# A linear-attention and FFN kernel: float32 numerators on column halves of the array, and the key side and the denominators turned through DRAM

## The chip, the cores and the metric

One core of a Trainium2 chip runs the whole program. The metric is the device time of one execution in microseconds (us); lower is better.

## What is computed

```python
def phi(x):
    proj = np.einsum('bhsd,md->bhsm', x, omega)
    sq = np.sum(x * x, axis=-1, keepdims=True) / 2.0
    h = proj - sq
    h = h - np.max(h, axis=-1, keepdims=True)
    return np.exp(h) / np.sqrt(m)
q_p, k_p = phi(q * scale), phi(k * scale)
kv = np.einsum('bhsm,bhsd->bhmd', k_p, v)
z = np.sum(k_p, axis=2)
num = np.einsum('bhsm,bhmd->bhsd', q_p, kv)
den = np.einsum('bhsm,bhm->bhs', q_p, z)[..., None] + 1e-06
attn = num / den                       # 8 batches, 8 heads, 576 tokens, 64 wide, 128 features
x = attn.transpose(0, 2, 1, 3).reshape(4608, 512)
h = x @ w_in                           # 512 x 2048
return (h - np.tanh(h)) @ w_out        # 2048 x 512
```

## The kernel before

The 4608 tokens are cut into eleven chunks of 256, 256, 256, 384, 384 and six times 512. For each chunk the FFN runs over 16 slices of 128 hidden columns: `h` (12 matmuls, L541), tanh on ACT (L815), a subtraction on DVE (L816), a split of the result into a high and a low part (L817 on ACT, L818 on DVE), and 3 matmuls for each of the chunk's 128-token blocks into `po` (L564 to L566). Every product of full accuracy in the FFN is made of three passes in `float32r`, a one-pass format: high by high, high by low, low by high.

The attention of a later chunk is woven into the FFN of an earlier one. Heads are handled in pairs, c = 0 to 3, two heads of 64 rows side by side in 128 partitions. Three kinds of units make it:

- Batches 0 to 2 and chunks 0 to 2 go through `native_k` and `native_q`, in plain float32, in the first part of the program (the table `ORDER`). `native_q.pn` (L1019) multiplies two heads into the two column halves of the array, rows 0 to 63 and 64 to 127 of one PSUM bank.
- Each batch b = 3 to 7 and pair c is a `k_unit` (20 in all). It makes the features of the keys, splits them and the values, and adds up kv transposed in a bank `pk`. Then it sums z per partition on DVE (`zA` to `zl`, L732 to L749), and PE turns both: `kt` (L760, L762) makes two transposes, and two matmuls against ones that add z up over the partitions and spread it over all of them. `ka`, `kb` and `zb` read that back out of PSUM, `wa` and `wv` split kv into two halves for the numerators.
- Each chunk 3 to 10 and pair c is a `q_unit` (32 in all), written `q<chunk><pair>` in the tables. Per 128-token block it projects (`p`, L593), copies and reduces (`c`, `t`), takes the exponential (`e`, L612) and sums the denominators (`d`, L623). Then `r` takes the reciprocal, `n` multiplies the features by it on ACT (L632), `tr` turns 32 x 32 blocks on DVE (L635), four DMAs `dw` write them to DRAM and two DMAs `dr` read them back with tokens along the free axis (L641, L644). Per head, `a` (L654, ACT) and `l` (L658, DVE) split the features into a high and a low part, `m` (`numerators`) makes the products, and `ta` (L670, ACT) and `tv` (L674, DVE) add the two parts of the product into `xs`, the chunk's input to the FFN. `xh` and `xl` split that into `xa`.

A chunk crosses a batch edge at most once (576 tokens are four and a half blocks), so `numerators` runs over one or two pieces of a chunk, and per piece and head it makes two `float32r` matmuls, one of `qh` and one of `ql`, each with all 128 columns of `kvw` (64 of the high part of kv, 64 of the low).

The order of all work is written out by hand in two tables, `ORDER` and `LATER`; a token is `unit.step.slot`, and each engine runs its instructions in that order. `LATER` begins near 170 us. SP issues nearly all DMAs, one after the other; a DMA that has to wait holds up those behind it. Engines: PE matmuls, DVE and ACT elementwise work, SP the DMAs.

Of the kernel before, what the change touches and what calls it, by code (L numbers as in the profile page):

```python
# [9 lines left out]
F32 = mybir.dt.float32  # L10
# [43 lines left out]
k23.exp5.1 q11.pt1.4 k13.kvwa k13.kvwd k00.pk0.2 k11.red5 q11.qt1.1 k10.lk.1 q01.nA1 k11.redB q11.pn.7 k11.redA  # L54
# [5 lines left out]
k10.exp5.1 d0.di k23.kvwa k23.zb k12.pj.1.7.5 q01.qt0.1 q10.expB.7 k23.kvwd k01.z k01.zt q10.expA.4 k12.redB  # L60
# [28 lines left out]
f0f.h0.6 f0e.gl q31.ld k30.sv0 q30.c0.0 f0f.h1 k30.sv1 k30.vhA0.0 k30.vhA1.1 q30.t0 k31.ld q30.e0 k30.vlA0 q30.p1.4  # L89
k30.vlA1 q30.p2.7 q30.d0 k30.pA0.0 f0f.th f0e.o0 x.h0 f0f.g x.h1 f0e.o1 x.h2 x.l0 f0f.gh x.l1 f0e.o2 x.l2 x.h3 f0f.gl  # L90
q30.c1 f0e.o3 q30.c2 q31.sa x.l3 q30.t1 f20.h0.6 q30.t2 q30.e1 q31.sv q30.e2 f20.h1 k30.cA0.0 q30.d1 q32.ld q30.d2
k30.tA0 q31.p0.4 f20.th q31.p1.7 q30.r q31.p2.0 q30.n0 f0f.o0 f20.g q30.n1 f0f.o1 q30.tr0 f20.gh q30.tr1 f0f.o2 s0.c0.2
s0.c1.3 q30.dw0 f0f.o3 q31.c0.1 q30.dw1 f20.gl s0.c2.1 s0.d0 f21.h0.6 q31.c1 s0.d1 q31.t0 q31.c2 s0.d2 q31.e0 s0.c3.0
q30.dw2 q30.dw3 q32.sa q31.d0 s0.d3 f21.h1 q31.t1 q31.t2 q31.e1 q32.sv q31.e2 k30.pA1.4 k30.pM.7 f20.o0.2 f21.th q31.d1
q33.ld k30.eA0 f21.g k30.cA1 f20.o1.3 q30.dr0 q31.d2 k30.cM.0 f21.gh q30.dr1 k30.khA0.0 q31.r k30.tA1 q31.n0 f21.gl
f22.h0.6 q31.n1 q31.tr0 k30.eA1 q31.tr1 k30.klA0 f22.h1 q31.dw0 k30.khA1.1 q31.dw1 k30.tM k30.klA1 q30.a0 q31.dw2
k30.zA.0 q31.dw3 k30.eM q30.l0 f21.o0 f22.th k30.zA2 k30.zM f22.g f21.o1 f22.gh f22.gl q30.m0.0 k30.pB0.4 q30.ta0.2
# [12 lines left out]
k30.kb k31.klA1 q33.dr1 k30.wa f27.h1 k31.khM.0 k30.wv k31.klM k31.vlM k31.zA.0 k31.zA2 q32.m1.7 f27.th k31.zM q40.p0.4  # L110
k31.kvA1 q30.xh f27.g k31.kvM f26.o0 q31.xh q30.xl q40.c0.0 f27.gh q31.xl q33.a0 q40.t0 f26.o1 q40.e0 f27.gl k31.vhB0.0
q33.l0 k31.vhB1.1 q40.p1.4 q32.ta1 q40.d0 f30.h0.6 k31.vlB0 q40.c1 k31.vlB1 q40.t1 k32.lv q40.e1 q32.tv1 q33.m0.4
q40.d1 q32.xh q40.p2.7 q33.a1 q32.xl q40.c2 q33.l1 q41.sa q40.t2 q41.sv q33.m1.7 q33.ta0.0 q33.ta1 q33.tv0 q40.e2
q42.ld q40.d2 q41.p0.4 q41.c0.1 q33.tv1 q40.r q33.xh q41.p1.7 q41.t0 q40.n0 q33.xl q41.p2.4 q40.n1 q40.tr0 f30.h1
q41.e0 q40.tr1 q41.c1 q41.d0 f27.o0 q40.dw0 q41.c2 q41.t1 q40.dw1 f30.th q40.dw2 q41.t2 q41.e1 q40.dw3 f30.g q41.e2
f27.o1 q41.d1 f30.gh q41.d2 s2.c0.2 f30.gl k31.pB0.7 q42.sa s2.c1.3 s2.d0 k31.pB1.4 f31.h0.6 q41.r s2.d1 q42.sv q41.n0
f31.h1 q41.n1 q40.dr0 q41.tr0 k31.cB0.0 q40.dr1 k31.cB1 f30.o0.2 q41.tr1 q43.ld f31.th k31.tB0 k32.sa q41.dw0 f30.o1.3
f31.g q41.dw1 f30.o2.1 q41.dw2 k31.tB1 q41.dw3 k32.sv0 f31.gh f32.h0.6 k31.eB0 f31.gl q40.a0 f32.h1 k31.khB0.0 k31.eB1
k32.sv1 f31.o0 q40.l0 k33.ld f32.th k31.klB0 f31.o1 f32.g q40.m0.7 q41.dr0 k31.khB1.1 f32.gh k31.zB.0 q41.dr1 k31.kvB0
f31.o2 k31.klB1 q40.a1 f32.gl k32.vhA0.0 k31.kvB1 q40.ta0.1 q40.l1 f33.h0.6 k32.vhA1.1 q40.tv0 k31.zB2 k32.vlA0 f33.h1  # L120
k31.ca.0 k32.vlA1 k31.zM2 k31.cv q40.m1.4 k31.zh.0 f33.th k31.zl q42.p0.7 q41.a0 f32.o0 f33.g q42.c0.0 q41.l0 f32.o1
# [248 lines left out]
def favor_attention_ffn(ctx: ExitStack, tc: tile.TileContext, qT, kT, va, vt, omT, w, out):  # L370
# [202 lines left out]
    def q_unit(ch, c):  # L573
# [75 lines left out]
        def rows_of(x):  # L649
            return x.rearrange("p (t a j) -> p t a j", a=4, t=T)  # L650
# [559 lines left out]
```

## Time and profile before

| what | us |
|---|---|
| three runs | 1016.25, 1025.86, 1025.47 (median 1025.47) |
| the profiled execution | 1017.37 |
| its span, first to last instruction | 1015.6 |

Around the profiled span lie 1.8 us that no instruction fills. The profile is of one execution; what a row calls busy is the union of its instructions, and a matmul's listed duration contains the time in which its results drain, so that matmuls that follow each other overlap. The time from one matmul's start to the next one's start is what it takes of PE.

### The profile page before, as it was taken

What the parts mean: (1) busy time and instruction counts of PE and PEld (TensorE: products, weight loads), DVE (VectorE), ACT (ScalarE), POOL (GpSimd) and SP (SyncE); (2) the same over time, 40 slices, a digit from 0 to 9 for tenths busy, and PEclk for the clock granted to TensorE, in tenths of its full rate; (3) what the DMA queues carried; (4) which work ended last, traced back from release to release, by engine and by line L of the source; (5) the groups of instructions that cost most, each with busy time, mean ns of one, the idle gap of its engine ahead of it and who ended that gap; (6) DMA issues with size and microseconds to landing.
All of it is one profiled execution on the core that took longest, in us unless ns stands there. A gap on an engine that the chain in (4) does not pass through costs nothing.

```text
span 1015.6 us, 16915 instructions
## 1 busy us (share of the span) xinstructions
PE 993.8 (98%) x5260; PEld 839.8 (83%) x5260; DVE 802.5 (79%) x2844; ACT 730.3 (72%) x1905; POOL 49.5 (5%) x77
## 2 busy tenths in 40 slices
PE   8999999989999999999999999999999999999998
PEld 7878778978889888888887888888888888888886
DVE  6999778998999999999998998898898638424222
ACT  8997668888888887888887886877778638323222
POOL 1334330000000000000000000000000000000000
PEclk9999999999999999999999999999999999999999
DMA  8888883333323334132323233232312311101001
GB/s 266 238 226 240 196 217 104 81 90 103 97 75 97 87 96 121 44 111 53 95 72 94 60 81 117 53 89 77 107 38 75 76 63 45 40 1 42 0 1 42
DMA packets 71962, 96.71 MB, mean 95 GB/s; under 512 B 14272, under 2 KB 43840, under 8 KB 71872
## 3 DMA queue, kind: packets, MB, share of 16 engines
q1 hardware_dynamic: 64400, 69.78, 24.7%
q10 hardware_dynamic: 5168, 17.47, 5.2%
q0 software_dynamic: 2304, 8.39, 4.4%
q8 instruction: 42, 0.69, 0.3%
q14 instruction: 48, 0.39, 0.1%
HBM read 62.05 MB, written 25.17 MB: 86 GB/s over the span
## 4 chain that ended last, share of the span: by engine, by line
PE 61%; DVE 18%; ACT 12%; issue 3%; DMA 3%; POOL 0%; ACTq 0%; SPq 0%; DVEq 0%; POOLq 0%
PE h L541 26%; PE po L566 8%; PE po L564 8%; PE po L565 8%; ACT phi_q L632 4%; PE pj_q L593 2%; PE pk L728 2%; DVE zf L816 2%; DVE zr L818 1%; DVE phi_q L605 1%; PE k_pk L915 1%; DVE zf L623 1%; PE pn L665 1%; ACT phi_q L612 1%; PE pn L664 1%
## 5 line engine op out<-in xcount | busy, mean ns | idle before, releaser
L541 PE MATMUL h<-xa,w 128*128 128x512 f32 (+2 forms) x1920 | 422.1, 369 | 1.3 <-DVE zf L552 1.0
L541 PEld LDWEIGHTS h<-xa,w 128*128 128x128 f32 x1920 | 340.9, 189 | 55.4 <-DVE zf L816 1.5
L564 PE MATMUL po<-w,zr 128*128 128x512 f32 x544 | 213.8, 393 | 1.2 <-ACT zr L554 1.2
L566 PE MATMUL po<-w,zr 128*128 128x512 f32 x544 | 213.5, 392 | 0.5 <-DVE zr L556 0.4
L565 PE MATMUL po<-w,zr 128*128 128x512 f32 x544 | 213.4, 392 | 0.0
L815 ACT ACTIVATE zf<-h 128x512 f32<-128x512 f32 (+1 forms) x138 | 78.2, 567 | 142.8 <-PE h L541 138.3
L816 DVE TENSOR_TENSOR zf<-h,zf 128x512 f32<-128x512 f32 (+1 forms) x138 | 90.4, 655 | 114.3 <-ACT zf L815 113.1
L566 PEld LDWEIGHTS po<-w,zr 128*128 128x128 f32 x544 | 102.5, 188 | 23.7 <-DVE zr L556 1.4
L564 PEld LDWEIGHTS po<-w,zr 128*128 128x128 f32 x544 | 102.7, 189 | 18.1 <-ACT zr L554 1.4
L565 PEld LDWEIGHTS po<-w,zr 128*128 128x128 f32 x544 | 102.6, 189 | 16.4
L818 DVE TENSOR_TENSOR zr<-zf,zr 128x512 fp32r<-128x512 f32 (+1 forms) x138 | 90.5, 656 | 21.0 <-ACT zr L817 19.7
L817 ACT CAST zr<-zf 128x512 fp32r<-128x512 f32 (+1 forms) x138 | 82.2, 596 | 31.0 <-DVE zf L816 30.0
L612 ACT ACTIVATE phi_q<-phi_q,nb_q 128x128 f32<-128x128 f32 x240 | 80.8, 393 | 18.1 <-DVE nb_q L605 17.2
L632 ACT ACTIVATE phi_q<-phi_q,dn 128x128 f32<-128x128 f32 x240 | 74.5, 390 | 13.6 <-DVE dn L628 13.3
L635 DVE STREAM_TRANSPOSE phi_q<-phi_q 128x512 f32<-128x512 f32 (+1 forms) x64 | 43.2, 677 | 18.6 <-ACT phi_q L632 18.0
L605 DVE CUSTOM_DVE_ANT_1 phi_q<-pj_q,phi_q 128x128 f32<-128x128 f32 x240 | 57.3, 283 | 0.3
L623 DVE CUSTOM_DVE_ANT_0 zf<-phi_q,zb 128x128 f32<-128x128 f32 (+1 forms) x200 | 49.7, 285 | 1.3 <-ACT phi_q L612 0.9
L593 PE MATMUL pj_q<-om,qx 128*128 128x256 f32 x240 | 46.8, 293 | 3.6 <-DVE zf L674 1.8
L593 PEld LDWEIGHTS pj_q<-om,qx 128*128 128x128 f32 x240 | 37.9, 190 | 10.8 <-issue 2.7
L600 ACT COPY phi_q<-pj_q 128x256 f32<-128x256 f32 x120 | 41.1, 371 | 2.4 <-PE pj_q L593 2.1
L658 DVE TENSOR_TENSOR ql<-phi_q,qh 128x512 fp32r<-128x512 f32 (+1 forms) x64 | 41.6, 650 | 0.4
L654 ACT CAST qh<-phi_q 128x512 fp32r<-128x512 f32 (+1 forms) x64 | 37.5, 587 | 0.6 <-DMA phi_q<-turned 0.4
(177 smaller groups left out, 1513.8 us busy)
## 6 DMA issues: line engine op xcount, KB each, us to landing
raw<-w ACTq DMA_DIRECT2D x32, 512.0 KB, 5.5
turned<-phi_q SPq DMA_DIRECT2D x96, 128.0 KB, 2.6
phi_q<-turned SPq DMA_DIRECT2D x48, 256.0 KB, 2.9
w<-a POOLq DMA_DIRECT2D x16, 512.0 KB, 5.8
v<-vt SPq DMA_DIRECT2D x20, 320.0 KB, 3.0
qf<-qT SPq DMA_DIRECT2D x24, 256.0 KB, 2.7
kf<-kT SPq DMA_DIRECT2D x20, 288.0 KB, 2.9
out<-xs SPq DMA_DIRECT2D x18, 256.0 KB, 2.0
```

The lines of the kernel that those rows point to most:

```text
L541: nc.tensor.matmul(o, w_, x, start=i == 0, stop=i == len(prods) - 1)
L564: nc.tensor.matmul(po[t], gh[:, 2 * j + t], wt[f][:, 0, DM:], start=first, stop=False)
L565: nc.tensor.matmul(po[t], gh[:, 2 * j + t], wt[f][:, 1, DM:], start=False, stop=False)
L566: nc.tensor.matmul(po[t], gl[:, 2 * j + t], wt[f][:, 0, DM:], start=False, stop=last)
L593: nc.tensor.matmul(u["pj", t][:, h], u["x"][:, h, t * P : (t + 1) * P], om2, start=True, stop=True)
L605: nc.vector.tensor_tensor_reduce(u["ph"][:, h, :, t], quarters(u["pj", t][:, h, :M]), u["ph"][:, h, :, t], scale=-SCALE, scalar=3.0e38, op ...
L612: nc.scalar.activation(ph, ph, AF.Exp, bias=u["nb", t][:, h : h + 1], scale=-1.0)
L632: nc.scalar.activation(u["ph"][:, h, :, t], u["ph"][:, h, :, t], AF.Copy, scale=u["dn"][:, 2 * t + h : 2 * t + h + 1])
L815: th=lambda: nc.scalar.activation(g, blocks(u["p"])[:, 0:n], AF.Tanh),
L816: g=lambda: nc.vector.tensor_sub(g, blocks(u["p"])[:, 0:n], g),
L817: gh=lambda: nc.scalar.copy(gh, g),
L818: gl=lambda: nc.vector.tensor_sub(gl, g, gh.bitcast(F32)))
```

## The change

Four things change.

1. `numerators` works in plain float32: one matmul per head, piece and run of blocks, 64 columns of kv each, head 0 into rows 0 to 63 of one bank and head 1 into rows 64 to 127. It reads the turned features where they lie (runs of 32 elements), so the split `a`, `l` is gone, and with it the buffers `qh` and `ql`; a third buffer `phq2` takes part of their room. A piece that ends in the middle of a block is cut into up to three runs.
2. The features are no longer multiplied by 1/den (`n` is gone). 1/den is turned by DVE in 32 columns (`rt`), written to DRAM in four DMAs of 6 or 8 rows of 128 B (`rw`), and read back by two DMAs (`rr`), each of which gives one head's row to 64 partitions of `xs`. `xm` multiplies the numerators in PSUM by it, one DVE instruction in place of `ta` and `tv`.
3. In a `k_unit` PE no longer turns anything: `tr` turns kv and z on DVE, four DMAs write them to DRAM, one reads them back (`dr`), `zr` sums z, `zt` turns it, four small DMAs `rw` write it and one DMA `zb` reads it into all 128 partitions. `kb` adds the two halves of kv, `wv` (ACT) copies the result.
4. `kvw` is float32 with 128 columns in place of 256 in halves; in `ORDER` the eight steps `kvwd` (L938) fall away. `LATER` is written anew, every step of it.

```diff
-        def norm(h):
-            for t in range(T):
-                nc.scalar.activation(u["ph"][:, h, :, t], u["ph"][:, h, :, t], AF.Copy, scale=u["dn"][:, 2 * t + h : 2 * t + h + 1])
...
-        def q_hi(h): ...
-        def q_lo(h): ...
-                nc.tensor.matmul(u["pn", h][:, s:e], w, u["qh", h][:, s:e], start=True, stop=False)
-                nc.tensor.matmul(u["pn", h][:, s:e], w, u["ql", h][:, s:e], start=False, stop=True)
-        def x_part(*slot, h): ...
-        def x_sum(h): ...
+        def numerators(slot):
+            u["pn"] = ps.tile([P, TW], F32, tag=BANKS[slot], name=f"pn_{n}")[:, :L]
+            to = u["pn"].rearrange("p (t a j) -> p t a j", a=4, t=T)
             for b, s, e in pieces:
+                for t0_, t1, a0_, a1 in parts(s, e):
+                    for h in range(2):
+                        nc.tensor.matmul(to[D * h : D * h + D, t0_:t1, a0_:a1], kvs[b, c][0][:, h], in_order(h)[:, t0_:t1, a0_:a1],
+                                         start=True, stop=True)
+        def r_turn():
+            nc.vector.transpose(u["rt"], u["all"])
+        def put_r(a):
+            nc.sync.dma_start(u["rd"].rearrange("h t (a j) -> a (h t) j", a=4)[a], u["rt"][32 * a : 32 * a + 2 * T])
+        def get_r(slot):
+            u["xs"] = xs[slot][:, :T]
+            for h in range(2):
+                nc.sync.dma_start(u["xs"][D * h : D * h + D].rearrange("p t j -> p (t j)"),
+                                  u["rd"][h].rearrange("(o t) p -> o (t p)", o=1).to_broadcast([D, L]))
+        def over():
+            nc.vector.tensor_mul(u["xs"], blocks(u["pn"]), u["xs"])
...
-        def turned():
-            for h in range(2):
-                nc.tensor.transpose(u["pk"][:, 0, h], u["c"][:, h], ident)
-            for i in range(2):
-                nc.tensor.matmul(u["pk"][:, 1].rearrange("p h m -> p (h m)"), ones, ...
+        def turn():
+            nc.vector.transpose(c, c)
+        def get():
+            nc.sync.dma_start(u["cz"].rearrange("p a q j -> p (a q j)"), u["dr"].rearrange("p a q j -> p (a q j)"))
+        def z_sum():
+            nc.vector.tensor_reduce(u["z"][:, 0:2], u["cz"][:, :, 2:4].rearrange("p a h j -> p h a j"), axis=AX.XY, op=ALU.add)
+        def put_z(a):
+            nc.sync.dma_start(u["zd"].rearrange("h (a j) -> a h j", a=4)[a], u["zt"][32 * a : 32 * a + 2])
         def zb():
-            nc.scalar.copy(u["zb"], u["pk"][:, 1])
+            nc.sync.dma_start(u["zb"].rearrange("p h m -> p (h m)"), u["zd"].rearrange("(o h) m -> o (h m)", o=1).to_broadcast([P, 2 * M]))
...
 LATER, the end of chunk 3's last unit:
-q42.ld q40.d2 q41.p0.4 q41.c0.1 q33.tv1 q40.r q33.xh q41.p1.7 q41.t0 q40.n0 q33.xl q41.p2.4 q40.n1 q40.tr0 f30.h1
+q32.xl f30.h0.6 q33.xl q42.c2 q41.dr0 k30.tr k31.cA0.0 k31.cA1 q41.dr1 f30.h1 q42.t2 k30.dw0 q42.e2 k31.tA1 k30.dw1
```

The program has 721 DMAs on SP, where it had 329.

What stands on PE at the end of chunk 3's attention, before the first `h` of chunk 3 (`pn_3_3` are the numerators of the unit of chunk 3 and pair 3, `h_3_0` is the first slice of chunk 3's FFN). Before:

```order
L664 MATMUL pn_3_3_0_2746<-qh_3_3_0_2701,k13_kvw_459 128x384
L665 MATMUL pn_3_3_0_2746<-ql_3_3_0_2717,k13_kvw_459 128x384
L593 MATMUL pj_q4_0_2_2752<-om_91,qx_4_0_2481 128x256 x2
L664 MATMUL pn_3_3_1_2769<-qh_3_3_1_2755,k13_kvw_459 128x384
L665 MATMUL pn_3_3_1_2769<-ql_3_3_1_2759,k13_kvw_459 128x384
L593 MATMUL pj_q4_1_0_2781<-om_91,qx_4_1_2761 128x256 x2
L593 MATMUL pj_q4_1_1_2789<-om_91,qx_4_1_2761 128x256 x2
L593 MATMUL pj_q4_1_2_2799<-om_91,qx_4_1_2761 128x256 x2
L541 MATMUL h_3_0_2728<-xa_96,w0_651 128x384 x6
```

The first six matmuls of `h_3_0` stand just ahead of these rows. Now, from the same numerators on:

```order
L540 MATMUL h_2_6_2558<-xa_96,w12_1624 128x256 x12
L540 MATMUL h_2_6_2558<-xa_96,w13_1675 128x256 x12
L663 MATMUL pn_3_3_2607<-phi_q3_3_2306,k13_kvw_459 64x384 x2
L592 MATMUL pj_q4_1_2_2616<-om_91,qx_4_1_2442 128x256 x2
L736 MATMUL pk_3_0_2093<-khl_3_0_B0_2537,vhl_3_0_B0_2218 128x256 x2
L736 MATMUL pk_3_0_2093<-khl_3_0_B1_2554,vhl_3_0_B1_2222 128x256 x2
L563 MATMUL po_2_0_2103<-w10_1447,zr_67 128x512
L564 MATMUL po_2_0_2103<-w10_1447,zr_67 128x512
```

`h_3_0` comes 31 rows further on; from `pn_3_3` to it there are 24 matmuls of 512 columns and 40 of 256. The last numerators of chunk 3 have moved from between the two halves of the matmuls that need them to well ahead.

What stands on SP in the same stretch (`turned` is the DRAM copy of the features, `over` that of 1/den). Before:

```order
L641 DMA turned_3_3_2577<-phi_q3_3_2374 64x4x96 x4
L644 DMA phi_q3_3_2374<-turned_3_3_2577 128x384 x2
L696 DMA v_3_2_2741<-vt 128x640
L581 DMA qf_4_2_2777<-qT 128x384
L641 DMA turned_4_0_2825<-phi_q4_0_2697 64x4x96 x4
```

Now:

```order
L638 DMA turned_3_3_2458<-phi_q3_3_2306 64x4x96 x4
L673 DMA over_3_3_2489<-rt_3_3_2463 6x32 x4
L580 DMA qf_4_2_2518<-qT 128x384
L641 DMA phi_q3_3_2306<-turned_3_3_2458 128x384 x2
L638 DMA turned_4_0_2541<-phi_q4_0_2407 64x4x96
L673 DMA over_4_0_2552<-rt_4_0_2543 6x32
L678 DMA zf_68<-over_3_3_2489 64x384 x2
L673 DMA over_4_0_2552<-rt_4_0_2543 6x32 x3
L638 DMA turned_4_0_2541<-phi_q4_0_2407 64x4x96 x3
```

Each unit now has six DMAs more in the queue, and the writes of the next unit stand between the writes and the reads of this one.

## Rows read from the trace of the kernel before

**Rows 1.** The page's first line: busy us of each engine, its share of the span, and instructions.

```profile
PE 993.8 (98%) x5260; PEld 839.8 (83%) x5260; DVE 802.5 (79%) x2844; ACT 730.3 (72%) x1905; POOL 49.5 (5%) x77
```

**Rows 2.** Stretches of the span: length, busy us of PE, PEld, DVE, ACT and POOL with instruction counts, granted TensorE clock (1.00 is 2.4 GHz), DMA share, GB/s.

```profile
215.00:225.00 10.00, 7.03 (x37) 5.50 (x36) 9.71 (x38) 8.83 (x23) 0.00 (x0) 1.00 0.19 62
225.00:230.00 5.00, 4.28 (x14) 3.73 (x15) 4.38 (x24) 4.20 (x14) 0.00 (x0) 0.58 0.14 41
230.00:240.00 10.00, 10.00 (x47) 8.82 (x46) 7.97 (x30) 8.48 (x24) 0.00 (x0) 0.87 0.66 177
240.00:890.00 650.00, 644.05 (x3218) 546.07 (x3217) 567.32 (x2185) 504.05 (x1370) 0.00 (x0) 1.00 0.29 78
890.00:1015.00 125.00, 121.59 (x537) 100.35 (x535) 35.38 (x52) 31.71 (x53) 0.00 (x0) 1.00 0.05 17
```

**Rows 3.** What PE waited for from 215 to 235 us: total us, times, longest.

```profile
PE pj_q L593 <- DVE zf L674: 1.8, 2, 1.1
PE pn L664 <- ACT qx L438: 1.7, 1, 1.7
```

**Rows 4.** PE in order of time: start us, us, what. First the numerators of one head in chunk 3, then chunk 5 (a batch edge after 192 tokens), chunk 9 (after 448) and chunk 10 (none); the first row of each and what follows the last.

```profile
245.69 0.34 PE L664 MATMUL pn<-qh,k_kvw 128*128 128x384 f32 x1
...
246.05 0.40 PE L593 MATMUL pj_q<-om,qx 128*128 128x256 f32 x2
...
347.71 0.25 PE L664 MATMUL pn<-qh,k_kvw 128*128 128x192 f32 x1
...
348.23 0.39 PE L564 MATMUL po<-w,zr 128*128 128x512 f32 x1
348.46 0.40 PE L565 MATMUL po<-w,zr 128*128 128x512 f32 x1
...
790.79 0.37 PE L664 MATMUL pn<-qh,kvw 128*128 128x448 f32 x1
...
791.34 0.48 PE L564 MATMUL po<-w,zr 128*128 128x512 f32 x1
791.66 0.40 PE L565 MATMUL po<-w,zr 128*128 128x512 f32 x1
...
836.63 0.40 PE L664 MATMUL pn<-qh,kvw 128*128 128x512 f32 x1
...
837.10 0.40 PE L564 MATMUL po<-w,zr 128*128 128x512 f32 x1
```

**Rows 5.** PE in order of time around one `kt` of a `k_unit`.

```profile
466.79 0.38 PE L760 MATMUL pk<-zf,c 128*128 128x128 f32 x2
466.92 0.48 PE L762 MATMUL pk<-zhl,ones 128*128 128x256 f32 x2
467.24 0.40 PE L454 MATMUL pj_k_A<-om,kx 128*128 128x256 f32 x2
```

**Rows 6.** PE in order of time around one `native_q.pn`, float32 on column halves (16 records for 512 tokens of two heads), between matmuls of the FFN; and the group of its 256-column records over the whole span (busy us, mean ns of one).

```profile
144.61 1.07 PE L541 MATMUL h<-xa,w 128*128 128x512 f32 x4
145.61 1.10 PE L1019 MATMUL q_pn<-q_qt,kvf 128*64 128x64 f32 x16
146.64 1.21 PE L541 MATMUL h<-xa,w 128*128 128x512 f32 x4
...
L1019 PE MATMUL q_pn<-q_qt,kvf 128*64 128x256 f32 x32 | 4.3, 392 | 0.3 <-ACT q_qt L1012 0.2
```

**Rows 7.** Groups of instructions by line: busy us, mean ns of one, then idle time before them and what ended it.

```profile
L632 ACT ACTIVATE phi_q<-phi_q,dn 128x128 f32<-128x128 f32 x240 | 74.5, 390 | 13.6 <-DVE dn L628 13.3
L635 DVE STREAM_TRANSPOSE phi_q<-phi_q 128x512 f32<-128x512 f32 (+1 forms) x64 | 43.2, 677 | 18.6 <-ACT phi_q L632 18.0
L658 DVE TENSOR_TENSOR ql<-phi_q,qh 128x512 fp32r<-128x512 f32 (+1 forms) x64 | 41.6, 650 | 0.4
L654 ACT CAST qh<-phi_q 128x512 fp32r<-128x512 f32 (+1 forms) x64 | 37.5, 587 | 0.6 <-DMA phi_q<-turned 0.4
L674 DVE TENSOR_TENSOR zf<-pn,zf 64x512 f32<-64x512 f32 (+1 forms) x32 | 20.9, 653 | 4.2 <-ACT zf L670 3.7
L670 ACT COPY xs<-pn 64x512 f32<-64x512 f32 (+1 forms) x32 | 17.8, 555 | 5.8 <-PE pn L665 5.2
L749 DVE TENSOR_TENSOR zhl<-zs,zhl 128x256 fp32r<-128x256 f32 x20 | 8.4, 418 | 0.2
```

**Rows 8.** DMA issues (KB each, median us from issue to landing); SP in order of time (x4 and x2 are issued one behind the other); SP's own wait between write and read (us, times, longest); ACT's wait for a read from 176 to 890 us.

```profile
raw<-w ACTq DMA_DIRECT2D x32, 512.0 KB, 5.5
turned<-phi_q SPq DMA_DIRECT2D x96, 128.0 KB, 2.6
phi_q<-turned SPq DMA_DIRECT2D x48, 256.0 KB, 2.9
out<-xs SPq DMA_DIRECT2D x18, 256.0 KB, 2.0
...
392.75 2.56 SPq L641 DMA_DIRECT2D turned<-phi_q  x4
398.22 0.81 SPq L644 DMA_DIRECT2D phi_q<-turned  x2
...
SPq L644 <- DMA turned<-phi_q: 44.9, 40, 2.0
ACT qh L654 <- DMA phi_q<-turned: 0.4, 1, 0.4
```

More of the change, by code (lines that the diff above doesn't have):

```diff
@@ L93 @@
[L93 to L97, printed above, removed]
@@ L568, in favor_attention_ffn @@
     pos = {}
+    columns = []
     dram = ctx.enter_context(tc.tile_pool(name="dram", bufs=4, space=bass.MemoryType.DRAM))
-    zsum_tile = []
     x2 = {}
@@ L615, in den @@
             if t == 0:
-                u["dn"] = sb.tile([P, 2 * WB], F32, tag="dn", name=f"dn_{n}", bufs=8)[:, : 2 * T]
+                columns.append(columns.pop(0))
+                u["all"] = columns[-1]
+                u["dn"] = u["all"][:, : 2 * T]
             for b, s, e in pieces:
@@ L619, in den @@
                 for h in range(2):
-                    i = 2 * t + h
+                    i = h * T + t
                     if s < e:
@@ L672, in x_sum, with parts @@
-        def x_sum(h):
-            r = slice(D * h, D * h + D)
-            nc.vector.tensor_add(u["xs"][r], blocks(u["pn", h])[r], u["xs"][r])
-        st = dict(ld=ld, sa=sa, r=recip, sv=lambda: split_lo(u["x"], u["f"]), xh=lambda: x_hi(ch, c, u["xs"]), xl=lambda: x_lo(ch, c, u["xs"]))
+        def parts(s, e):
+            out = []
+            if s % P:
+                out.append((s // P, s // P + 1, 2, 4))
+                s += P // 2
+            if s // P < e // P:
+                out.append((s // P, e // P, 0, 4))
+            if e % P:
+                out.append((e // P, e // P + 1, 0, 2))
+            return out
@@ L677, in q_unit @@
+        def over():
+            nc.vector.tensor_mul(u["xs"], blocks(u["pn"]), u["xs"])
+        st = dict(ld=ld, sa=sa, r=recip, sv=lambda: split_lo(u["x"], u["f"]), xh=lambda: x_hi(ch, c, u["xs"]), xl=lambda: x_lo(ch, c, u["xs"]),
+                  m=numerators, rt=r_turn, rr=get_r, xm=over)
         for t in range(T):
@@ L680, in q_unit @@
         for a in range(4):
-            st[f"dw{a}"] = partial(put, a)
+            st[f"dw{a}"], st[f"rw{a}"] = partial(put, a), partial(put_r, a)
         for h in range(2):
-            for k, f in dict(n=norm, tr=turn, dr=get, a=q_hi, l=q_lo, m=numerators, ta=x_part, tv=x_sum).items():
+            for k, f in dict(tr=turn, dr=get).items():
                 st[f"{k}{h}"] = partial(f, h=h)
@@ L791, in k_unit @@
             st["kv" + g] = partial(kv, g=g)
-        st.update(zA=partial(zsum, h=0), zB=partial(zsum, h=1), zA2=partial(zsum2, 0), zB2=partial(zsum2, 1),
-                  zM=partial(z_mid, 0), zM2=partial(z_mid, 1), zh=z_hi, zl=z_lo, ca=c_hi, cv=c_sum, kt=turned,
-                  ka=lambda: nc.scalar.copy(kvt, u["pk"][:, 0, :, D:]),
-                  kb=lambda: nc.vector.tensor_add(kvt, u["pk"][:, 0, :, 0:D], kvt), zb=zb, wa=w_hi, wv=w_lo)
+        st.update(zA=partial(zsum, h=0), zB=lambda: zsum(0, 1), zA2=partial(zsum2, 0), zB2=partial(zsum2, 1), zM=partial(z_mid, 0),
+                  zM2=partial(z_mid, 1), ca=c_hi, cv=c_sum, tr=turn, dr=get, zr=z_sum, zt=z_turn, zb=zb, kb=kv_sum, wv=weights)
+        for a in range(4):
+            st[f"dw{a}"], st[f"rw{a}"] = partial(put, a), partial(put_z, a)
         return st
@@ L1159, in favor_attention_ffn @@
         xs += [ak.tile([P, TW // P, P], F32, name=f"xs{i}") for i in (2, 3)]
-        zsum_tile.append(ak.tile([P, 2, M], F32, name="zs"))
+        for i in range(6):
+            columns.append(ak.tile([P, 32], F32, name=f"columns{i}"))
+            nc.gpsimd.memset(columns[i], 0.0)
         for tag, kb, dtype in PLACES:
```

661 lines of the change are left out of this document (331 added, 330 removed).

## The prediction

> **What bounds the kernel now.** The page's first line comes first: PE is busy 98% of the span, DVE 79%, ACT 72% [rows 1]. The table of stretches then shows that this is no average over unlike stages. From 240 to 890 us, where all later attention runs, PE is busy 644.05 of 650 us while DVE has 567.32 and ACT 504.05 [rows 2]. So a microsecond taken from ACT or DVE is worth nothing by itself; what counts is what PE has to do, and the few places where PE waits. One such place stands out: from 215 to 230 us PE is idle 2.97 + 0.72 us, and the clock column falls to 0.58 and then 0.87 [rows 2]. What ended those waits were the `qx` of the next unit on ACT and the `xs` sum L674 on DVE [rows 3], that is, the numerators of chunk 3 come late, just when its FFN wants them.
>
> **The change on PE, numerators.** I take start-to-start times. Before, one head costs 0.36 us in chunk 3 (245.69 to 246.05) and the same in 4, 0.52 in chunk 5 (and its mirror 7), and 0.47 in chunk 10. In chunk 9 it is 0.55, plus 0.09 because the matmul behind the last short one takes 0.32 in place of 0.23 [rows 4]. For chunks 6 and 8, whose edges lie between, I put 0.49 and 0.58. Twice the sum over eight chunks is 7.86 us per pair c, and times four pairs 31.4 us.
>
> After, the shape is that of `native_q.pn`: plain float32, two heads in the column halves. Its 32 records of 256 columns list 392 ns each, 12.5 us in a row, yet their union is 4.3 us [rows 6]: records of the two heads run beside each other. From 145.61 to 146.64 one such group of 512 tokens takes 1.03 us. On top, the four matmuls ahead need 1.00 us from their start to the group where 4 x 0.23 = 0.92 would do, and the four behind list 1.21 in place of 1.07 [rows 6]. So one group costs 1.03 + 0.08 + 0.14 = 1.25 us. Two heads of one unit are no cheaper in plain float32 than in two `float32r` passes (1.25 against 0.94 to 1.28), and the going in and out of the halves is paid on each of the 32 calls. I take 1.25 for the six chunks of 512. For 384 tokens I take off 128 columns: if some 0.15 us of the group's 1.03 are entry and exit (an estimate, twice the 0.08 seen ahead of it), 0.88 us over 512 tokens is 1.7 ns each, 0.21 us less; that gives 1.04. Per pair 2 x 1.04 + 6 x 1.25 = 9.58, times four 38.3 us. **Numerators: +6.9 us** (range +3 to +9 if entry and exit differ from this one place; the new runs of 32 elements in the moving operand have no row, see the rivals).
>
> Here two rules of the Trainium skill pull apart. "TensorE: Matmul & The Clock Gate", in the part on packing small matmuls, says that outputs in separate column groups let matmuls run side by side; by that alone the two heads would cost about 0.9 us and the numerators would save 2 us. "TensorEngine Tiling (Array Packing)", under key properties, says that a change of the tiling mode drains the engine, which speaks against this change. By it each of the 32 calls pays the drain twice, and the trace agrees with about 0.2 to 0.37 us per call.
>
> **The change on PE, `kt`.** 466.79 to 467.24 is 0.45 us for two transposes and two sums against ones [rows 5], and there are 20: **-9.0 us**. Nothing on PE takes their place. Both terms together: PE has 2.1 us less to do. All FFN matmuls, projections and `pk` stay.
>
> **ACT and DVE.** ACT loses L632 (74.5 us), L654 (37.5) and both halves of L670 (2 x 17.8), some 148 us [rows 7]. DVE loses L658 (41.6), two L674 (2 x 20.9), L749 (8.4) and its cast, some 97. It gains 32 `xm` at 0.65 (20.9), 20 turns of 512 columns at about 0.70 (14), 52 turns of 32 columns and 20 sums `zr` over 256 elements. No row shows the last two: the small turn lies between nothing and 0.68 [rows 7], I take 0.2; `zr` I take at L749's 0.42. That is 54 us, so DVE ends 43 us lower. Since PE covers both engines nearly everywhere, I count neither as time. What they give back is PE's waits, in two parts.
>
> **Chunk 3's end.** The order now puts `pn_3_3` 24 matmuls of 512 columns and 40 of 256 ahead of `h_3_0`, about 24 x 0.23 + 40 x 0.12 = 10 us; before, the second head's stood 0.7 us ahead of the half that needs them. And the chain is shorter: `m`, `xm`, `xh`, `xl` in place of `a`, `l`, `m`, `ta`, `tv`, twice. PE's idle 3.7 us there, and the lower clock, should go. At 1.2 GHz work takes twice as long: 0.42 x 5 and 0.13 x 10 us below full [rows 2] are 2.1 + 1.3 = 3.4 us lost. **-6 of 7.1 us**, since some wait may stay; the bounds are 0 and -7.1. What is late next there is DVE, busy 9.71 of 10 us from 215 to 225 [rows 2].
>
> **Other waits.** PE idles 5.95 us more from 240 to 890 [rows 2], and the pipelined ends hide short gaps. DVE's wait for L632 before each turn (18.0 us [rows 7]) goes with L632, and neither the 64 pairs of L664 and L665 nor the 20 `kt` wait for a split any more. I take **-3 us** (0 to -8).
>
> **New waits.** 392 more DMAs go through SP. Four writes take 2.56 us to issue and two reads 0.81; a write lands after 2.6 us, a read after 2.9 [rows 8]. So a q unit adds about 2.5 + 0.8 us on SP, a k unit about 5; over 720 us SP issues for 40% of the time. From `rw` to `xm` the least is 4 x 0.35 + 2.6 + 0.8 + 2.9 = 7.7 us. SP already reaches `dr` early and waits 44.9 us in 40 times, yet ACT waited only once for what it read, 0.4 us [rows 8]: the table leaves just enough room. Counting the PE work between the tokens of the new table with the durations above, `rr` stands 2.9 to 7.9 us ahead of `xm` (median 4.5), the last `rw` 3.0 us or more ahead of `rr`, and `dr` 3.4 us or more ahead of `m`. DVE, and with it `xm`, `zr` and the first `d` behind `zb`, now waits directly for DMAs, 72 times; behind a late `xm` stand the subtractions and splits of the FFN, for which PE waits. I take **+2 us**. The read of one 1.5 or 2 KB row into 64 partitions, or of 1 KB into 128, has no row: 2.0 us (256 KB out) from below, 5.5 (512 KB in) from above [rows 8]; I take 2.9, as `dr` is nearest.
>
> "DMA: Bandwidth & Descriptors" of the Trainium skill (rules for kernel authors) says that transfers under 64 KB are mostly overhead and should be merged. The writes of 1/den are 1 KB. By its fixed 2 us per transfer `rw` would land 0.6 us sooner than I count, which no run here shows and which moves no term.
>
> **Sum.** -2.1 - 6 - 3 + 2 = -9.1 us against the profiled execution's 1017.37, which gives 1008.3. The runs lie on two levels, 1016 and twice 1025.5, and the profile is on the lower; no row says what parts them. Against the median of 1025.47 the same change gives 1016.4. If the upper level comes from the stretch at 215 to 240 us (one more fall of the clock there), it goes too, and the median would be near 1008. I put 0.2 on that, which moves the forecast to **1015 us**.
>
> **Rivals.**
> *Only PE's sum.* The new order makes a wait of its own as long as chunk 3's: DVE was full there and stays nearly as full. Then -2.1 and little else: 1021 to 1025, no change that can be measured (a measurement here tells about 1%). For it: DVE's load per microsecond falls by only 7%, and the table fills it again. Against it: the 10 us in the order.
> *The rows read back come late (slower).* Place: `xm`, and `d` behind `zb`. If a read into 64 partitions from one line of DRAM lands after more than 4.5 us, half the `xm` are late; at 5.5 us they and the `zb` are late by 1.5 us on average, 52 x 1.5 = 78 us of DVE waiting. DVE has 83 us free from 240 to 890 [rows 2], but not at these places; I give PE half, +39, so 1055 at the end of the bound and 1034 at 4.5 us. For it: SP holds up all behind a waiting DMA and now has twice as many. Against: all reads of 192 to 256 KB land in 2.9 us.
> *The column halves do not run beside each other, or the strided operand streams at half speed.* The change then doesn't do what it says on PE: 27 us more of streaming, about 1040. Against: rows 6. The 32-element runs alone are not shown there.
>
> **Chances and range.** Forecast with its spread 0.57 (of it 0.38 faster by over 1%, 0.19 within), with the upper level gone 0.08 (faster), only PE's sum 0.2 (within), late rows 0.1 and slow halves 0.05 (slower). Faster 0.46, same 0.39, slower 0.15. The range runs from 1000 (all waits and the upper level gone, no new wait: 1017.4 - 2.1 - 7.1 - 8) to 1033 (the late rows at 4.5 us); the forecast's own is 1006 to 1023.
>
> **What would show it.** Right: 1.2 to 1.3 us from the first L663 of a unit to the matmul after it, with entry and exit; no clock below 0.95 between 200 and 250 us; PE busy over 98.5% from 240 to 890; `xm` waiting for DMAs under 5 us in all. Wrong: `zf<-over` or `zb<-zd` landing after 4 us, DVE waits for DMAs over 20 us, or L663 groups of 2 us.

## The result, and the profile after

| | before | after |
|---|---|---|
| median of the runs | 1021.6 us (4 runs, 1016.25 to 1025.86) | 993.4 us (4 runs, 992.21 to 993.88) |
| span of the profiled execution | 1015.6 us | 990.4 us |
| ratio | | 0.9725, 95% interval 0.9665 to 0.9784 |

The forecast was 1015 us, with a range from 1000 to 1033: the sign was right, the size was not, and 993.4 lies below the range. Span against span 25.2 us are gone where the sum had 9.1. Two of the four runs of before stand near 1025 us; against the other two, 1016.25 and 1017.73, the change gains 24 us.

The page's first line (busy us, share, instructions), beside [rows 1]:

```profile
PE 976.7 (99%) x5260; PEld 810.1 (82%) x5260; DVE 749.2 (76%) x2772; ACT 592.1 (60%) x1497; POOL 48.9 (5%) x83
```

ACT has 138 us less (forecast 148) and DVE 53 (forecast 43). The stretches that answer to [rows 2], columns as there:

```profile
215.00:225.00 10.00, 10.00 (x60) 8.38 (x59) 9.94 (x50) 8.64 (x23) 0.00 (x0) 1.00 0.62 160
225.00:230.00 5.00, 5.00 (x28) 3.89 (x27) 4.90 (x14) 1.03 (x4) 0.00 (x0) 1.00 0.62 174
230.00:240.00 10.00, 9.64 (x51) 8.28 (x50) 7.51 (x33) 6.61 (x19) 0.00 (x0) 1.00 0.62 188
240.00:890.00 650.00, 648.06 (x3294) 536.91 (x3293) 520.29 (x2096) 383.23 (x1009) 0.00 (x0) 1.00 0.39 106
```

PE is full at chunk 3's end, and nothing answers to [rows 3]. From 240 to 890 us PE's busy time grew by only 4 us, yet 76 more of its matmul records lie in the stretch. PE now runs in order of time like this around numerators (start us, us, what), first for 384 tokens and then for 512 with no batch edge, beside [rows 4]:

```profile
222.69 0.87 PE L663 MATMUL pn<-phi_q,k_kvw 128*64 128x384 f32 x4
223.48 0.50 PE L563 MATMUL po<-w,zr 128*128 128x512 f32 x1
223.82 0.39 PE L564 MATMUL po<-w,zr 128*128 128x512 f32 x1
...
760.45 1.08 PE L663 MATMUL pn<-phi_q,kvw 128*64 128x512 f32 x4
761.46 0.50 PE L563 MATMUL po<-w,zr 128*128 128x512 f32 x1
```

The matmul behind a group starts 0.79 or 1.01 us after the group does and itself takes 0.34 in place of 0.23; 0.09 are lost ahead of the group. That is 0.99 us for 384 tokens and 1.21 for 512; forecast were 1.04 and 1.25.

The new work on DVE, by line (busy us, mean ns of one, idle time before it and what ended that):

```profile
L632 DVE STREAM_TRANSPOSE phi_q<-phi_q 128x512 f32<-128x512 f32 (+1 forms) x64 | 40.3, 650 | 0.1
L783 DVE TENSOR_REDUCE columns<-cz 128x2 f32<-128x256 f32 x20 | 8.2, 412 | 0.2
L668 DVE STREAM_TRANSPOSE rt<-columns 128x32 f32<-128x32 f32 x32 | 6.5, 203 | 0.0
```

What `xm` on DVE waited for the new transfers (us, times, longest):

```profile
DVE xs L682 <- DMA xs<-over: 3.6, 3, 1.4
DVE zf L682 <- DMA zf<-over: 1.1, 3, 0.4
DVE xs L682 <- DMA over<-rt: 0.6, 1, 0.6
```

The turn's 18 us of waiting for ACT [rows 7] are gone. The reads of 1/den came late 7 times in 32, by 5.3 us in all.

Where did 25 us come from? A busy share can't say it, since each matmul's listed duration covers the next one's start. So I added up, over the whole trace, the time from each matmul's start to the next one's, by kind (us; two of the experiments below stand beside it):

| from this kind's start to the next matmul's | before | after | before without n | before without kt |
|---|---|---|---|---|
| kt | 9.4 | 0 | 9.3 | 0 |
| numerators | 33.6 | 31.3 | 32.1 | 34.9 |
| projections of q | 37.2 | 32.4 | 35.3 | 38.1 |
| projections of k | 22.8 | 23.0 | 22.3 | 24.2 |
| pk, both kinds of units | 52.6 | 47.2 | 47.7 | 53.0 |
| h | 398.9 | 399.0 | 398.0 | 400.2 |
| po | 402.2 | 398.9 | 397.6 | 405.5 |
| other work of the first part | 53.3 | 53.2 | 55.5 | 54.0 |
| sum | 1010.0 | 985.0 | 997.8 | 1009.9 |

Much of the loss of before lay in matmuls that the change doesn't touch: projections of q, pk and po took 13.5 us more than they do after. With a matmul of 256 columns at 0.119 us, 384 at 0.174 and 512 at 0.227, these kinds, h and the projections of k held 31 us of waiting and of lowered clock before, and 18 after, 6 of which are the way into and out of the column halves (0.09 and 0.11 us at each of 32 calls). I call this the stock of hidden waits. Without n it is 18, too.

### The profile page after: what moved, and what is told of

It reads as the page before. It is cut to its first block, busy times and chain, and to the rows that moved or that the text cites. A ratio compares the mean times of both kernels' runs of the same rounds, so it can differ in the third digit from the quotient of the medians.

```text
span 990.4 us, 16846 instructions
## 1 busy us (share of the span) xinstructions
PE 976.7 (99%) x5260; PEld 810.1 (82%) x5260; DVE 749.2 (76%) x2772; ACT 592.1 (60%) x1497; POOL 48.9 (5%) x83
## 4 chain that ended last, share of the span: by engine, by line
PE 84%; DVE 7%; ACT 3%; DMA 3%; issue 1%; SPq 1%; POOL 0%; ACTq 0%; DVEq 0%; POOLq 0%
PE h L540 35%; PE po L563 11%; PE po L565 11%; PE po L564 11%; PE pn L663 3%; PE pj_q L592 3%; PE pk L736 2%; PE k_pk L944 1%; DMA xs<-over 1%; PE pj_k_B L453 1%; PE pj_k_A L453 1%; DMA raw<-w 1%; PE k_pj L921 1%; DVE zf L1015 1%; DVE a L1118 1%
## 5 line engine op out<-in xcount | busy, mean ns | idle before, releaser
L632 DVE STREAM_TRANSPOSE phi_q<-phi_q 128x512 f32<-128x512 f32 (+1 forms) x64 | 40.3, 650 | 0.1
L470 ACT ACTIVATE phi_kA<-phi_kA,nb_k_A 128x128 f32<-128x128 f32 x80 | 27.0, 394 | 16.9 <-DVE nb_k_A L464 16.7
L470 ACT ACTIVATE phi_kB<-phi_kB,nb_k_B 128x128 f32<-128x128 f32 x80 | 27.1, 394 | 5.5 <-DVE nb_k_B L464 5.4
L663 PE MATMUL pn<-phi_q,kvw 128*64 128x64 f32 (+4 forms) x224 | 24.7, 347 | 0.0
```

The lines of the kernel that those rows point to most:

```text
L663: nc.tensor.matmul(to[D * h : D * h + D, t0_:t1, a0_:a1], kvs[b, c][0][:, h], in_order(h)[:, t0_:t1, a0_:a1], start=True, stop=True)
```

## Experiments

Times are medians. The kernel before had 1017 to 1022 us beside each set; a ratio is against it, with its 95% interval. The expectations weigh three theories of why the gain is 16 us beyond the 9.1 of the prediction's sum: "load" (ACT and DVE have less to do), "order" (the new table has what PE needs ready earlier) and "chain" (n no longer stands between the exponentials and the turned features).

**1. Leaving out n, alone.** In the table of the order the 64 tokens `n0` and `n1` fall away:

```diff
-q33.r k30.vlB1 q33.n0 k31.tA0 f26.h1 k31.lv k31.tA1 q33.n1 q33.tr0 k31.eA0 q33.tr1
+q33.r k30.vlB1 k31.tA0 f26.h1 k31.lv k31.tA1 q33.tr0 k31.eA0 q33.tr1
```

> The kernel before with n left out, so the numerators aren't divided (this leaves out the division): 74.5 us less on ACT, and the DVE turn (18 us of waiting for n before) follows the sums directly; the order of all else is the old one. Load: half of the 16 us, -6 to -10 against before. Chain: the same or more, -6 to -12. Order: within 2 us of before.

Measured 1002.7 us, ratio 0.9858 (0.983 to 0.9885): 15 us from an engine whose time I had called worth nothing, and more than any of the three theories had. The stretch from 240 to 890 us:

```profile
240.00:890.00 650.00, 649.27 (x3276) 557.10 (x3274) 566.53 (x2190) 450.37 (x1171) 0.00 (x0) 1.00 0.29 78
```

All of PE's waits that are listed in it (us, times, longest):

```profile
PE pj_q L591 <- DVE qx L443: 0.2, 1, 0.2
PE pj_q L591 <- DVE nb_k_B L463: 0.2, 1, 0.2
```

PE is busy 649.27 of 650 us there, in the old order and with DVE as full as before (566.53 us, 567.32 in [rows 2]). The clock still falls at chunk 3's end (0.54 from 225 to 230 us), so the 15 us aren't that stretch.

**2. n's time without its waits.** n stays at its places but scales a constant tile into a scratch tile:

```diff
-                nc.scalar.activation(u["ph"][:, h, :, t], u["ph"][:, h, :, t], AF.Copy, scale=u["dn"][...])
+                nc.scalar.activation(scra, scri, AF.Copy, scale=1.0)
```

> The kernel before with n at its places on ACT, but scaling a constant tile into a scratch tile (this leaves out the division): ACT keeps its 74 us, while n no longer waits for the reciprocal and the turn no longer waits for n. If the 15 us that leaving out n gave are ACT's load: no gain, within 3 us of before (1015 to 1021). If they are the waits on the way of the features (theory 'chain'): the whole gain again, 1000 to 1006.

1014.5 us, 0.9967 (0.994 to 0.9993). The scalings take 74.5 us of ACT, as n did. Taken out in this order, the waits are 3 of the 15 us and n's time on ACT is 12.

**3. The same time elsewhere on ACT.** The scalings of experiment 2 behind `ta0` and `ta1`, in place of ahead of the turn:

```diff
-q33.r k30.vlB1 q33.n0 k31.tA0 f26.h1 k31.lv k31.tA1 q33.n1 q33.tr0
+q33.r k30.vlB1 k31.tA0 f26.h1 k31.lv k31.tA1 q33.tr0
...
-q33.ta0.0 q33.ta1 q33.tv0
+q33.ta0.0 q33.n0 q33.ta1 q33.n1 q33.tv0
```

> The kernel before with the idle scalings of the earlier run (a constant tile into a scratch tile; this leaves out the division), but taken from n's place ahead of the turn to behind the copies ta, four behind each. ACT has as much to do as there (1014.5). If ACT's load as such costs the 12 us: 1012 to 1017. If it is the place in ACT's order (leaving out ta's 36 us cost nothing): 1000 to 1005.

1045.7 us, 1.0274 (1.0249 to 1.0298): neither, 31 us worse than at n's own place. DVE's waits from 170 to 900 us show it, first with the scalings at n's place (experiment 2), then behind `ta`:

```profile
DVE ql L660 <- ACT qh L656: 2.3, 2, 1.7
DVE zf L625 <- ACT phi_q L614: 1.9, 6, 0.6
```

```profile
DVE ql L663 <- ACT qh L659: 12.7, 15, 1.2
DVE zf L628 <- ACT phi_q L617: 9.1, 11, 2.1
```

The four scalings now stand ahead of splits `a` (in 8 of the 32 units that of the next head, else of other units), exponentials and the FFN's tanh, and `a` and the exponentials come later than at n's place. PE's clock is at 1.2 GHz for 10.2, 6.8 and 6.8 us there, where with the scalings at n's place it was for 3.4 us once. What a microsecond on ACT costs hangs on what stands behind it in the fixed order.

**4. More off ACT.** n left out, and the copy of `ta` too (POOL sets two buffers of `xs` to zero once instead):

```diff
-            nc.scalar.copy(u["xs"][D * h : D * h + D], blocks(u["pn", h])[D - D * h : P - D * h])
```

> The kernel before with n and the 64 copies ta left out on ACT (this leaves out the division and one part of each product): ACT has some 110 us less in all. Theory 'ACT sets the pace': n alone gave 15 us, ta gives more, 994 to 999. Theory 'n was at a bad place': ta gives nothing more, 1001 to 1004.

1003.2 us, 0.9853 (0.9803 to 0.9903): `ta` gives nothing more. With n out PE has no listed waits left to lose (649.53 of 650 us from 240 to 890), and the stock of hidden waits stays at 18 us.

**5. kt off PE**, alone, with n out, and with n and `ta` out; the token goes, as in

```diff
-k31.vhA1.1 q32.m0.7 k30.kt k31.vlA1
+k31.vhA1.1 q32.m0.7 k31.vlA1
```

> The kernel before with the 80 matmuls of kt left out (ka, kb and zb then read what lies in the bank; this leaves out the transposes and the sum of z). If PE's work is the bound one for one: -9 to -11 us. If the waits fill the room that it leaves: -3 us or less.

> The kernel before with both n and kt left out (this leaves out the division, the transposes of kv and the sum of z). Alone, n gave 15 us and kt 2. Theory 'load, then PE' (ACT and DVE set the pace of the kernel before, and PE's work counts once they are relieved): kt is now worth most of its 9.4 us, 992 to 997. Theory 'load only' (PE's work never counts): 999 to 1003. Theory 'PE' (my forecast): kt worth its 9.4 us in both places, which the run without kt has already spoken against.

> The same with kt left out too. With n out alone kt was worth 2 us. If ACT sets the pace until it is relieved, PE's work begins to count with ta gone: kt worth 5 us or more, 988 to 994. If PE's work never counts in the old order: within 2 us of the run with kt.

1015.5 us, 0.9967 (0.9943 to 0.9992); 1000.7 us, 0.9851 (0.9821 to 0.988); 999.8 us, 0.9823 (0.9767 to 0.9879). The 9.4 us of PE's work give 2 us alone, 2 with n out and 3 with both out. The stretch from 240 to 890 us without kt:

```profile
240.00:890.00 650.00, 640.35 (x3151) 538.78 (x3151) 569.04 (x2187) 505.46 (x1374) 0.00 (x0) 1.00 0.30 78
```

PE's busy time fell from 644.05 [rows 2] to 640.35 and DVE's stayed: the room went into waits (table above: po, the numerators, h and the projections grew by what kt left). By the same sum the stock of hidden waits rises from 31 to 38 us with kt out alone, and from 18 to 24 with kt out behind n, or behind n and `ta`. "Load, then PE" had forecast 992 to 997 for the second and 988 to 994 for the third, so it falls: behind n and `ta` a third limit is near.

**6. l off DVE.** The 64 subtractions go, and the second matmul reads qh again:

```diff
-                nc.tensor.matmul(u["pn", h][:, s:e], w, u["ql", h][:, s:e], start=False, stop=True)
+                nc.tensor.matmul(u["pn", h][:, s:e], w, u["qh", h][:, s:e], start=False, stop=True)
```

> The kernel before with the 64 subtractions l on DVE left out; the second matmul reads qh again in place of ql, so PE does the same work (this leaves out the low part of the features). DVE has 41.6 us less. Load: DVE is the fuller engine (87% from 240 to 890 us), -6 to -15 us. If only ACT counted: within 3 us of before.

1017.9 us, 1.0001 (0.9971 to 1.0031): 41.6 us of the fullest of the two elementwise engines, worth nothing while n stands.

**7. Chunk 3's end relieved in the old order**: 12 matmuls of chunk 2 fill PE's gap.

```diff
-q40.p2.7 q33.a1 q32.xl q40.c2 q33.l1 q41.sa q40.t2 q41.sv q33.m1.7 ... q41.p0.4
+q40.p2.7 q33.a1 q32.xl q40.c2 q33.l1 q41.sa q40.t2 q41.sv f27.o0 q33.m1.7 ... f27.o1 q41.p0.4
```

> The kernel before with two of its work items moved: the last po of chunk 2 (two times 6 matmuls, 2 x 1.37 us) ahead of the last numerators of chunk 3 and of the projections behind them, where PE waited 3.7 us and the clock fell. If that stretch costs what I took (6 of 7.1 us): -4 to -7 us. If the waits come back right behind it: 0 to -2 us.

1016.2 us, 0.9999 (0.9979 to 1.0018, so within 2 us). The stretches, to be held against [rows 2]:

```profile
215.00:225.00 10.00, 9.49 (x49) 7.63 (x48) 9.71 (x38) 8.70 (x23) 0.00 (x0) 1.00 0.21 66
225.00:230.00 5.00, 2.58 (x14) 1.88 (x13) 4.37 (x22) 4.41 (x15) 0.00 (x0) 1.00 0.14 41
230.00:240.00 10.00, 8.88 (x44) 7.67 (x45) 9.45 (x35) 9.41 (x26) 0.00 (x0) 1.00 0.71 193
```

The clock no longer falls, and nothing is gained: PE is idle 0.51 + 2.42 + 1.12 = 4.05 us in place of 3.69, while DVE is busy 23.5 of 25. The reading that fits is that the stretch was as long as DVE and ACT needed, so that PE's lower clock lay inside it; which of the two set it was not tried. Its runs still scatter from 1013.5 to 1022.2 us.

**8. More work on PE in the changed kernel**, and less on DVE (the low parts of the values on POOL):

```diff
+                if 2 <= ch <= 7:
+                    nc.tensor.matmul(u["p"][:, : 2 * M], om[:, 0], om2, start=True, stop=True)
```

```diff
-            nc.vector.tensor_sub(v[:, :, 1], u["v"][:, v0 : v0 + 2], v[:, :, 0].bitcast(F32))
+            nc.gpsimd.tensor_sub(v[:, :, 1], u["v"][:, v0 : v0 + 2], v[:, :, 0].bitcast(F32))
```

> The changed kernel with one more matmul of 256 columns on PE ahead of each of 88 h slices of chunks 2 to 7, into the bank that h then overwrites: 88 x 0.119 = 10.5 us of work. Load, then PE: the changed kernel is bound by PE, so +9 to +11 us, 1002 to 1005. If ACT and DVE still set the pace: +4 us or less, below 998.

> The changed kernel with the low parts of the values (100 subtractions of 128x128, 28 us on DVE) on POOL, which is idle from 170 us on. Load: DVE's relief takes away part of PE's last 12 us of waits, -2 to -6 us, 987 to 991. Order: the same time within 2 us, or slower by some us if a subtraction on POOL takes so long that the products pk wait for it.

1000.8 us, 0.984 (0.9813 to 0.9867), and 999.2 us, 0.9794 (0.9749 to 0.984; its runs lie from 991.2 to 1005.6). PE's 10.5 us cost 7.4 against 993.4, where in the old order 9.4 us had given 2. The changed kernel feels PE's work, but that doesn't make PE its bound: there work was added, in the old kernel it was taken away, and added work on ACT and DVE costs time, too (experiment 9). The runs with 28 us off DVE whose clock stayed at full speed took 991.2 to 996.9, so nothing is gained there; the subtraction takes 0.52 us on POOL, 0.28 on DVE.

**9. Load put back into the changed kernel.** Idle work into a scratch tile: all of n's, a's and l's; n's alone; n's spread behind the exponentials; a quarter of n's; l's alone. In one run n is in the chain again, by 1.0. The edit is that of n's alone:

```diff
+        def norm(h):
+            for t in range(T):
+                nc.scalar.activation(scra, scri, AF.Copy, scale=one[:, 0:1])
```

> The changed kernel with idle work put back on ACT and DVE: at the places of the old n, a and l each q unit makes 8 scalings of 128x128 and three more on ACT and 8 subtractions of 128x128 on DVE, all into a scratch tile that nobody reads (about 130 us on ACT, some 45 us on DVE over the program). Nothing new is waited for. Theory 'load' (PE's waits went because ACT and DVE have less to do): the 16 us beyond my forecast come back, 1004 to 1010. Theory 'order' (they went because the new table has what PE needs ready earlier): at most 3 us, 993 to 997. Theory 'chain' (they went because n left the way from the exponentials to the turned features): as order, 993 to 997.

> The same 240 scalings at the same places on ACT, but into a scratch tile; no turn waits for them. Load: as the run with n in the chain, 997 to 1001. Chain: no change, 992 to 996. Order: no change, 992 to 996.

> The changed kernel with n put back: the features are multiplied in place by 1.0 on ACT ahead of each DVE turn (240 instructions of 128x128, some 94 us on ACT), so the turn waits for ACT again. The result is unchanged. Load: +4 to +8 us, as ACT has two thirds of its old work back, 997 to 1001. Order: within 2 us, 992 to 996. Chain: +8 us or more, above 1001, since the features come 3 us later per unit and the least distances of the table are about 3 us.

> The changed kernel with the 240 idle scalings of the run into scratch, but spread: two behind each block's exponentials in place of four ahead of each turn. If the 41 us are the sum of the load on a full ACT: again 1028 to 1040. If they come from four in a row that stand ahead of the FFN's tanh and split in an engine's fixed order: under 15 us, 995 to 1008.

> The changed kernel with 64 idle scalings on ACT in place of 240, one ahead of each turn: 26 us of ACT work, where 96 us cost 41 us. If the load costs in proportion: +10 to +12 us, 1003 to 1006. If the new table has room for a small part: under 4 us, 992 to 997.

> The changed kernel with 128 idle subtractions of 128x128 on DVE, four ahead of each unit's numerators: 37 us of DVE work alone, as much as l was. In the kernel before l's 41.6 us were worth nothing. If DVE has no part in the pace: within 3 us, 991 to 996. If DVE is as tight as ACT in the new table: +12 us or more, above 1005.

In the order of these expectations: 1094.6 (all), 1034.6 (n's alone), 1048.3 (in the chain), 1041.7 (spread), 1002.4 (a quarter) and 1021.4 us (l's alone). The first two are far over every theory, the third over all but the open end of "chain"; spreading changed nothing for the better, a quarter came near a cost in proportion, and l's alone costs as if DVE were tight. The idle work took 135 us of ACT and 70 of DVE in the first run, 96 of ACT in the second. But the matmuls of h were slower even from 900 to 980 us, where there is no attention (count | busy us, mean ns), in the changed kernel and in the run with a quarter:

```profile
L540 PE MATMUL h<-xa,w 128*128 128x512 f32 x177 | 42.6, 389 | 0.0
```

```profile
L546 PE MATMUL h<-xa,w 128*128 128x512 f32 x172 | 42.6, 396 | 0.0
```

In the same busy time there are five fewer. All six runs had a new tile of 4 bytes per partition, `one`, and the run in the chain had no other. So the run with a quarter was made again without it (and without its 512-byte input tile, for which a part of `om` stands in):

```diff
-                nc.scalar.activation(scra, scri, AF.Copy, scale=one[:, 0:1])
+                nc.scalar.activation(scra, scri, AF.Copy, scale=1.0)
```

> The changed kernel with the same 64 idle scalings as the run with a quarter, but without its tile of 4 bytes per partition: the factor is a constant, the input an existing tile, the scratch 512 bytes. In all runs with the 4-byte tile the 512-column matmuls of h took 233.5 ns in place of 226.7 even where ACT and DVE are idle. If that tile's shift of the tiles behind it is the cause, and the new table has room for 26 us of ACT work: 992 to 996, with h at 226.7 ns. If ACT's work costs in proportion: again 1000 to 1004.

993.7 us, 0.9771 (0.975 to 0.9793), and h back at its old pace:

```profile
L546 PE MATMUL h<-xa,w 128*128 128x512 f32 x180 | 43.2, 389 | 0.0
```

So without the tile the run is 8.7 us shorter (1002.4 - 993.7); from start to start h alone takes 7.7 us less (398.7 in place of 406.4). The scalings by a constant are shorter, too, 308 ns in place of 400, so the 26 us of ACT have become 20; these cost nothing. Less 8.7, n's full load costs some 32 us, spread 40, in the chain 46, l's load on DVE 19, and all together 92. The new table has room for 20 us on ACT, not for all of n, and spreading doesn't help. Whether DVE has less room than ACT these runs don't show, since the amounts and the places differ.

## Why the prediction was wrong

**The step that failed** is in the first part: "a microsecond taken from ACT or DVE is worth nothing by itself; what counts is what PE has to do". I read it from PE's 98% [rows 1] and 644.05 of 650 us [rows 2]. Both halves are wrong for the kernel before: 74.5 us of ACT were worth 15 (experiment 1), and 9.4 us of PE were worth 2 (experiment 5). From that sentence came the term that was mis-sized: *other waits*, -3 with -8 as the bound. It measured about -15: of the 25.2 us of span `kt` gave 9.4 and the numerators cost 5.9, which leaves 21.7 for waits, and even with all 7.1 for chunk 3's end 14.6 are other waits, net of the new ones. I had written beside it that the pipelined ends hide short gaps, and still took the 5.95 us that are not hidden for the stock; from start to start the stock was 31 us, and some 4 more in the numerators and `kt` themselves.

The Trainium skill, "Perfetto Trace Analysis", in the section on the most-contended engine, says that the busy share of matmuls is not a good measure of how close a kernel is to its roofline (the limit that the hardware sets), because matmuls are pipelined. Here the trace agrees: 644.05 us of 650 looked full, and without n PE did more in the same 650 us (3276 records in place of 3218).

**Point by point.**

- *Numerators*: 32 calls at 0.99 to 1.24 us are 38.1 us with one wait, where 38.3 were forecast; the two heads do run beside each other, and going in and out costs what one place of the trace had said (with no wait they are 37.3, where those of before had 31.4 so). By the rule of the Trainium skill, "TensorEngine Tiling (Array Packing)", key properties, that a change of the tiling mode drains the engine, the trace agrees with 0.09 + 0.11 us around each call. The 2 us that the prediction lets the column halves alone save take 0.9 us for every call; with 0.66 us for 384 tokens and 0.88 for 512, from its own 1.7 ns per column, they would be 5. The sum doesn't use them.
- *kt*: PE's 9.4 us went, but by experiment 5 that alone gives 2.
- *Chunk 3's end*: waits and the fall of the clock went as forecast, but that this is worth 6 us is not shown: in the old order the clock's fall could be taken out for nothing (experiment 7). At 1.2 GHz a matmul of 512 columns took 0.427 us in place of 0.227, so "twice as long" is 1.9 times.
- *ACT and DVE*: sizes right to 10 us, `rt` 0.20 and `zr` 0.41 us as taken; "I count neither as time" is the failed step again.
- *New waits*: 5.3 us on DVE for the reads behind `xm`; PE's listed waits for `xm` are 1.6 us, which fits the +2.
- *Signs*: the 1.21 us of a group, the clock and PE's 99.7% came as signs of being right, and `xm` waited 5.3 us where under 5 was asked. None of them measured the other waits, so they could come true beside a wrong size.
- *Upper level*: I put 0.2 on the stretch at 215 to 240 us as the cause of the runs at 1025 us; experiment 7 speaks against it. In the profiles of four of the runs above the clock is low in the first 50 us, which are nearly the same in all these kernels. Here is the run without l, and behind it the kernel before (columns as in [rows 2]):

```profile
0.00:50.00 50.00, 47.84 (x378) 42.21 (x380) 28.98 (x90) 34.60 (x109) 7.78 (x26) 0.76 0.63 204
0.00:50.00 50.00, 46.10 (x462) 39.80 (x463) 37.76 (x123) 43.17 (x143) 12.29 (x34) 1.00 0.80 253
```

A mean granted clock of 0.76 of 2.4 GHz: 24 us of the stretch ran at 1.2, with 378 matmul records in place of 462. Of the kernel with the low parts on POOL the execution with such a fall took 1005.6 us, those at full clock 991.2 to 996.9. And of the runs of the kernel before beside the experiments, those with a mean granted clock of 0.994 or more took 1014.3 to 1018.6 us, those with 0.990 or less 1020.8 to 1030.5 (three outliers over 1200 us are left aside). So this fall probably made the 1025 us; no profile of the kernel before caught it.

**What holds in its place.** The reading that fits the runs is that in the kernel before three things stood nearly level: n's place in ACT's order, PE's work, and the rest of what PE waits for on DVE and ACT. Taking l or kt alone gives 0 to 2 us, since n holds the end; taking n gives 15, and then PE has no listed waits; taking `ta` too gives nothing, and taking kt too gives 2 to 3, since a third limit stands there. The change takes from all of them at once. Shown are: 15 us by n alone, 12 of them its time on ACT at that place; that PE's work gives little as long as the rest stays; that the changed kernel feels PE's work (7.4 of 10.5 us).

**Open.** Without n the old kernel stands at 1002.7 us, the changed one at 993.4. How these 9 us divide between kt, `a`, `l`, `ta` and `tv`, +5.9 us of numerators and the new table wasn't separated: the old table can't order the new steps. By the table of starts most of it is `kt`: 9.3 of the 12.8 us between the sums 997.8 and 985.0, and in the new order the stock of hidden waits stays at 18 us where in the old one it rose to 24. That DVE is the third limit was not run by itself (no run takes n and l out together). The traces point at it: by the semaphores' events, what released the late matmuls from 240 to 890 us was DVE for 13.9 of 19 us before, and for 7.2 of 12 with n and `kt` out. And none of the kernels tried beats the changed one: the run with a quarter of idle work (993.7) is level with it.

## What to carry to other kernels

Where engines run fixed orders and hand work to each other, an engine that is 98% busy is not yet the bound: add up the time from start to start of its instructions by kind, hold it against the shortest of the same shape, and look for waiting in groups that the change doesn't touch. Before a price is put on an edit, ask what would be late next if only this edit were made; when several engines are nearly level, most single edits give little (here 0, 2 and 15 us) and the set gives more than a sum over the fullest one says. A microsecond of an off-path engine costs by what stands behind it in its order: the same 64 sets of scalings cost 12 us at one place and 43 at another.

## What the hardware showed

A tile of 4 bytes per partition, allocated ahead of others, made the 512-column matmuls of h 3% slower (233.5 ns from start to start in place of 226.7, in the last 80 us) and those of po 1% (228.5 in place of 226.7); the run with a quarter was 8.7 us shorter without it, with 6 us less work on ACT. Six runs with the tile and all others without it agree on the pace of h, and in one of the six it is the only new tile. Which operand's place in memory does it was not tried. An experiment that adds a tile has to be read for that first.
